# Seven-product keys and values from the third pair of tiles, with the weight sums made earlier and the later key features scaled on GpSimd

## The chip, the cores and the metric

One core of a Trainium2 chip runs the kernel. The metric is the device time of one execution in microseconds. In the profile PE is TensorE (matmuls), DVE is VectorE, ACT is ScalarE, POOL is GpSimd and SP is SyncE, which here issues most DMAs; PEld is TensorE's loading of weights. Each engine works through its own queue of instructions in order, and waits at an instruction until the semaphores that it names have come.

## The reference

The input `x` has 2048 tokens of 512 features. Everything is float32.

```python
xn = (x - mean(x)) / sqrt(var(x) + 1e-5)               # per token

# A: linear attention with learned features, 32 heads of 16
q, k, v = split(xn @ wqkv)
pq, pk  = q @ w_phi, k @ w_phi                          # per head
phi_q   = concat(softmax(pq), softmax(-pq))             # 32 features a head
phi_k   = concat(softmax(pk), softmax(-pk))
kv, z   = sum over tokens of phi_k^T v, and of phi_k    # per head
s       = ((phi_q @ kv) / (phi_q . z + 1e-6)) @ wo

# B: gated feed-forward, F = 1376
gate = xn @ W_gate
ffn  = (gate * (gate > 0) * (xn @ W_up)) @ W_down

out = x + s * silu(ffn)
```

## The kernel before

**Products.** A float32 factor is split into a high and a low half, and each product is made of three matmuls: low by high, high by low, high by high (`mm3`). A projection of one tile of 128 tokens has four slices of the 512 inner rows, so 12 matmuls of 128x512.

**Phase 1.** The 16 tiles of tokens are read, normalised, transposed into `XT`, projected to keys and values, turned into key features, and summed into the state. Tiles 0 and 1 are set up one by one in a loop over `n in range(2)`. Then `pair(m)` runs for m = 1 to 7 with the tiles n = 2m and n + 1; below, "pair 3" is m = 3. On TensorE a pair is: keys of n, values of n + 1, the transposes of a later tile (`pxT`), a query product (`pq`), the state products (`pkv<-ek,v`) of the tiles n - 2 and n - 1, keys of n + 1, values of n, transposes, another query product.

**Two forms of a pair.** Four projections in the plain form are 48 matmuls. From the pair FIRST on, the four are made together by a scheme of seven products of half the inner depth, 7 blocks of 6, so 42 matmuls. The blocks use sums of token blocks (S1 to S4, which GpSimd and VectorE make for the feed-forward part anyhow: tiles `sb`, `xf`, `XT`) and four sums of the weights, `T[0]` to `T[3]`. Their order in a pair is: `py` from A11 by the weights themselves, `pz` from S1 by `T[0]`, `px` from S2 by `T[1]`, the rest of `py`, `px` from S3 by `T[2]`; then, after the state products, `px` from A22 by `T[3]` and the rest of `pz`. Between the blocks ScalarE copies partial sums out (`va`, `vb`) and VectorE adds them back into `v`.

**The weight sums.** `t_prep` defines the steps that make `T[0]` to `T[3]`. A step has a name of four characters: the engine (g GpSimd, s ScalarE), the operation (c combines weights in place, h copies the high half, l subtracts it to leave the low half), the number of the sum, and a slice. There are 20 steps on GpSimd, each a 128x512 operation writing `wvr`, `t`, `l` or `th`, and 8 on ScalarE. The dictionary PLAN places them: `t_steps(m, where)` stands at fixed places of `pair`, and the place decides where the step falls in its engine's queue. Pair 0 in PLAN is the set-up of tile 1.

**Key features.** `features_k(n, e, p, engine)` sums the exponentials `ek` on VectorE (`sm`), takes the reciprocal, and multiplies `ek` by it. Without an engine the reciprocal goes into the PSUM tile of the keys and VectorE multiplies; with one the reciprocal goes into a tile `rc` in SBUF and that engine multiplies. It is called twice in a pair: at its start for tile n - 1, and in its middle for tile n, just ahead of GpSimd's low halves of S1 and S3 (`sums_lo`) for tile n + 3.

**The sum of the features.** `features_split(n)` adds `ek` into `zacc` by a DMA that accumulates, 512 KB, issued by GpSimd. Each of these is made to wait, in GpSimd's queue, for the landing of the one before. There are 15. The state product of a tile needs its `ek` scaled; the products of `zacc` with `ones`, in the second tile of the feed-forward part, need the last accumulate landed.

**Order around it.** Everything is issued in the written order on each engine (line 60, the helper that records each instruction, so that nearly all instructions show as L60). A planner, `pace`, slips the preparation of the feed-forward weights (`f_prep`: tiles `rawg`, `wab`, `tab`, `wa`, `wb`, `wc`, `wd`, `fdh`, `fdl`) into the pairs 5 to 7 by its own estimate of free time: tile 2 first, then tiles 0 and 1; each product is stored to memory (`ws`) and fetched again later. In the pairs 1 to 4 SyncE spills parts of `XT` (`xts`). Behind pair 7 the feed-forward part begins with tile 0, and takes most of the rest of the time.

Of the kernel before, what the change touches and what calls it, by code (L numbers as in the profile page):

```python
# [33 lines left out]
         *(((q, j), (q + 1, j)) for q in (6, 4) for j in range(2)), ((3, 0), (3, 1))]  # L34
LAST = [2 * q + j for q in QUERIES[1] for j in range(2)][-3:]
AHEAD, AT = (2,), (10,)
FIRST = 4
PLAN = {(1, "end"): "gc51", (2, "start"): "gc01", (2, "sums"): "gc50 gc00", (2, "scaled"): "gc11", (2, "split a"): "sh01 gc21", (2, "turned"): "sh20", (2, "end"): "gc10 sh00 sh11", (3, "split b"): "sh21", (3, "sums"): "gl20 gc20", (3, "scaled"): "gl01", (3, "split a"): "gl00 gc31", (3, "turned"): "gl21 sh10 gc30", (3, "end"): "gl10", (4, "start"): "gl11 gc40 gc41", (4, "split b"): "sh30 sh31 gl31", (4, "sums"): "gl30"}

START = (14, 15)  # L40
WO_WITH = (4, 5, 6, 7)
# [119 lines left out]
def layer_kernel(ctx: ExitStack, tc: tile.TileContext, x, wkT, wqT, wv, wo, wf, cst, out):  # L161
    pace = Clock()
    nc = InOrder(tc, pace)
# [4 lines left out]
    def ps(shape=(P, 512), name="ps"):  # L168
        return pp.tile(list(shape), F32, tag="ps", name=name)
# [7 lines left out]
    def u2(shape, name, dt=F32):  # L177
        return sb.tile(list(shape), dt, tag="u2", bufs=B2, name=name)

    def small(n, name, bufs=3):  # L180
        return sb.tile([P, n], F32, tag=name, bufs=bufs, name=name)
# [7 lines left out]
    def add(engine, o, a, b, op=ALU.add):  # L189
        engine.tensor_tensor(o, a, b, op=op)  # L190
# [9 lines left out]
    def mm3(ps_out, w, m, ks, first=True, last=True):  # L200

        n = len(ks)
        for i, k in enumerate(ks):
            (wh, wl), (mh, ml) = w(k), m(k)
            mm(ps_out, wl, mh, first and i == 0, False)
            mm(ps_out, wh, ml, False, False)
            mm(ps_out, wh, mh, False, last and i == n - 1)
            if i < n - 1:
                pace.pump()
# [7 lines left out]
    def groups(e):  # L217
        return e.rearrange("p h s f -> p (h s) f")
# [23 lines left out]
    def rows(w):  # L242
        return lambda k: w[k]
# [35 lines left out]
    def norm_stats(*ns, bn=True):  # L279

        rs = small(2, "lr", 3)
        for k, n in enumerate(ns):
            STAT[n] = (norm_bn if k and bn else norm_sums)(n, rs[:, k:k + 1]), rs[:, k:k + 1]
        RS[ns] = rs

    def norm_scale(*ns):
        for n in ns:
            STAT[n][0][0]()
        rs = RS.pop(ns)[:, :len(ns)]
        nc.gpsimd.tensor_tensor(rs, rs, mhalf[:, :len(ns)], op=ALU.pow)  # L290

    def norm_apply(n):
        (_, m, sign), rs = STAT.pop(n)
        bias = small(1, "lb")
        nc.vector.tensor_scalar(bias, m, sign, rs, op0=ALU.mult, op1=ALU.mult)
        nc.scalar.activation(XN[n], XN[n], AF.Identity, bias=bias, scale=rs)
# [17 lines left out]
    def cols(n):  # L314
        i = order[n][1]
        return slice(i * P, (i + 1) * P)
# [56 lines left out]
    def xt_cols(n):  # L373
        a, c = A21 if n % 2 else A11, cols(n)
        return lambda k: (XT[:, a + k // 2, 0, k % 2, c], XT[:, a + k // 2, 1, k % 2, c])
# [3 lines left out]
    def spill_x(n):  # L379
        nc.sync.dma_start(xt_spill[:, :, :, :, cols(n)].rearrange("p c s k t -> p (c s k) t"),  # L380
                          f32(XT[:, 1:, :, :, cols(n)].rearrange("p c s k t -> p (c s k) t")))
# [37 lines left out]
    def exponents(pk):  # L419

        pkv_ = pk.rearrange("p (h f) -> p h f", f=DH)
        e = u4((P, H, 2, DH), "ek")
        mx = sb.tile([P, 2, H], F32, tag="mx", bufs=2, name="mx")
        nc.vector.tensor_reduce(mx[:, 0, :], pkv_, op=ALU.max, axis=AX.X)
        nc.vector.tensor_reduce(mx[:, 1, :], pkv_, op=ALU.min, axis=AX.X)
        for s in range(2):
            top = mx[:, s, :].unsqueeze(2).to_broadcast([P, H, DH])
            a, b = (top, pkv_) if s else (pkv_, top)
            nc.vector.tensor_tensor(e[:, :, s, :], a, b, op=ALU.subtract)
        return e  # L430
# [4 lines left out]
    def by_head(t, perm=False):  # L435

        return t.rearrange("p (c g f) -> p g c f" if perm else "p (g c f) -> p g c f", c=4, f=DH)
# [23 lines left out]
    def features_k(n, e, p, engine=None):  # L461

        sm = small(64, "sm", 2)
        nc.vector.tensor_reduce(sm, groups(e), op=ALU.add, axis=AX.X)
        rc = small(64, "rc", 2) if engine else p[:, 0:64]
        nc.vector.reciprocal(rc, sm)
        (engine or nc.vector).tensor_tensor(groups(e), groups(e), rc.unsqueeze(2).to_broadcast([P, 64, DH]), op=ALU.mult)
        EK[n] = e
# [5 lines left out]
    def features_split(n):  # L474
        phi = EK.pop(n)
        if n:
            nc.gpsimd.dma_start(zacc, flat(phi), accum_op=ALU.add)
        else:
            nc.sync.dma_start(zacc, flat(phi))
        PHI[n] = phi  # L480
# [636 lines left out]
    def t_steps(m, where):  # L1117
        for what in PLAN.get((m, where), "").split():
            STEPS[0](what)
# [66 lines left out]
    def pair(m):  # L1186

        n, c = 2 * m, cols(2 * m)
        at[0] = n

        def block(p, s, w, first):
            mm3(p, lambda k: (XT[:, s, 0, k, c], XT[:, s, 1, k, c]), rows(w), range(2), first)
            pace.pump()
        if m <= NP // 2:
            pace.later(4, lambda: spill_x(n - 1))
        seven = m >= FIRST
        py = ps(name="pk")
        if seven:
            block(py, A11, WK[:2], True)
            px = ps(name="pk")  # L1200
            nc.scalar.activation(px, py, AF.Copy)
        else:
            mm3(py, xt_cols(n), rows(WK), range(KD))
        if m > 1:
            features_k(n - 1, *EB.pop(), engine=MULT[1])
        t_steps(m, "start")
        pz = ps(name="pv")
        if seven:
            block(pz, S1, T[0], True)
            block(px, S2, T[1], False)  # L1210
            va = u2((P, D), "va")
            nc.scalar.activation(va, px, AF.Copy)
        else:
            mm3(pz, xt_cols(n + 1), rows(WV), range(KD))
        if m == 1:
            norm_apply(n + 4)
        else:
            features_split(n - 1)
        t_steps(m, "split b")
        news = [k for k in (n + 5, n + 6) if k < N]  # L1220
        if news:
            norm_stats(*news, bn=m > 2)
        if seven:
            block(py, A12, WK[2:], False)
        ea = exponents(py)
        if seven:
            block(px, S3, T[2], False)
            vb = u2((P, D), "vb")
            nc.scalar.activation(vb, px, AF.Copy)
            VH[n + 1] = u2((P, D), "v")  # L1230
            add(nc.vector, by_head(VH[n + 1], True), by_head(pz), by_head(vb))
        else:
            vb = pz
        t_steps(m, "sums")
        if news:
            norm_scale(*news)
        t_steps(m, "scaled")
        pace.pump()
        at[0] = n + 1
        if n + 3 < N:  # L1240
            t = turn(n + 3)
        exp_all(ea)
        if not seven:
            features_v(n + 1, vb)
        if n + 3 < N:
            turned(*t)
            sums_more(n + 3)
            sums_hi(n + 3, 0)
            if n + 7 < N:
                load_x(n + 7)  # L1250
        t_steps(m, "mid")
        query(n - 1)
        features_k(n, ea, py, engine=MULT[0])
        if n + 3 < N:
            sums_hi(n + 3, 1)
            sums_lo(n + 3)
        for k in news:
            norm_apply(k)
        pace.pump()
        features_split(n)  # L1260
        t_steps(m, "split a")
        kv_products(n - 2)
        kv_products(n - 1)
        pace.pump()
        if seven:
            block(px, A22, T[3], False)
        else:
            px = project(n + 1, WK, "pk")
        eb = exponents(px)
        if seven:  # L1270
            block(pz, S4, WV[2:], False)
            VH[n] = u2((P, D), "v")
            add(nc.vector, by_head(VH[n], True), by_head(pz), by_head(va))
        else:
            va = project(n, WV, "pv")
        if n + 4 < N:
            t = turn(n + 4)
            if n + 8 < N:
                load_x(n + 8)
        exp_all(eb)  # L1280
        t_steps(m, "turned")
        if n + 4 < N:
            turned(*t)
        if not seven:
            features_v(n, va)
        EB.append((eb, px))
        query(n)
        t_steps(m, "end")
        pace.pump()

    EB, MULT = [], [None, None]
    for m in range(1, NP):
        pair(m)
    features_k(N - 1, *EB.pop())
# [211 lines left out]
```

## Time and profile before

| | before |
|---|---|
| time, median of 3 runs | 549.36 us (548.53 to 551.20) |
| the profiled execution's own time | 548.27 us |
| its span | 546.5 us |
| PE busy | 540.7 us (99%) |
| POOL busy | 344.2 us (63%) |
| DVE busy | 377.2 us (69%) |
| ACT busy | 259.9 us (48%) |
| accumulates into `zacc` | 15, 512 KB each, median 5.9 us from issue to landing |

The span is the stretch between the first and the last instruction of the profiled execution; what lies around it, 1.8 us, is not in the trace. A row of a timeline gives the start in the span, the duration, the engine, the line, the operation with output and inputs, and in brackets the idle time of the engine ahead of it with what ended that. A duration can overlap the next instruction's, so the pitch of an engine is read from starts and ends of neighbours. A row of the windows gives for one stretch its length, then for each engine the busy time and the number of instructions, then TensorE's granted clock (1.00 is full), the DMA engines' share and GB/s.

### The profile page before, as it was taken

Reading aid. Unit: us, or ns where it says so; the run is one execution under the profiler, and the core shown is the slowest. Engines: PE = TensorE matmul, PEld = TensorE weight load, DVE = VectorE, ACT = ScalarE, POOL = GpSimd, SP = SyncE. Lnnn points to the kernel's source line nnn. Section 1 sums busy time; section 2 is a strip of 40 time slices with the busy share of each in tenths; the row PEclk is TensorE's granted clock in tenths of the full one; section 3 lists DMA queues with packets and bytes.
Section 4 is the critical chain, followed back from the end, with each engine's and each line's share of the span. In section 5 each row is a group of like instructions: output and inputs, shape, how many; then the busy total and the mean of one; then the engine's idle time right before and its main releaser. Section 6 shows DMA issues by size and latency. Waiting matters only on the chain.

```text
span 546.5 us, 9074 instructions
## 1 busy us (share of the span) xinstructions
PE 540.7 (99%) x3158; PEld 441.5 (81%) x3158; DVE 377.2 (69%) x582; ACT 259.9 (48%) x457; POOL 344.2 (63%) x311
## 2 busy tenths in 40 slices
PE   8999999999999999999999999999999999999997
PEld 8888887888877888878888888887877887878886
DVE  5978685897759486889833442899999494924323
ACT  3887666674622656455443241334354545342510
POOL 1665879477851999899976235262365765842591
PEclk9999999999999999999999999999999999999999
DMA  8349977659998548789696998792664734657073
GB/s 280 149 161 304 263 184 185 158 125 290 288 328 319 196 136 306 288 290 313 233 341 255 404 415 324 251 349 77 217 210 135 272 113 146 239 188 276 0 232 116
DMA packets 77518, 127.81 MB, mean 234 GB/s; under 512 B 6816, under 2 KB 29216, under 8 KB 76576
## 3 DMA queue, kind: packets, MB, share of 16 engines
q1 hardware_dynamic: 75168, 119.30, 62.1%
q0 software_dynamic: 2160, 7.87, 7.5%
q8 instruction: 25, 0.41, 0.3%
q14 instruction: 21, 0.17, 0.1%
q10 hardware_dynamic: 144, 0.07, 0.0%
HBM read 70.32 MB, written 48.50 MB: 217 GB/s over the span
## 4 chain that ended last, share of the span: by engine, by line
PE 84%; DVE 6%; POOL 5%; issue 2%; DMA 1%; ACT 1%; SPq 1%; ACTq 0%; POOLq 0%
PE py L60 20%; PE pd L60 9%; PE pa L60 9%; PE pb L60 8%; PE pso L60 8%; PE pk L60 7%; PE pq L60 6%; PE pc L60 6%; PE pv L60 4%; POOL l L60 2%; PE pnum L60 1%; PE pfold L60 1%; PE pkv L60 1%; PE pxT L60 1%; DMA wb<-ws 1%
## 5 line engine op out<-in xcount | busy, mean ns | idle before, releaser
L60 PE MATMUL py<-fdh,hl 128*128 128x512 f32 x176 | 68.9, 392 | 0.0
L60 PE MATMUL py<-fdl,hh 128*128 128x512 f32 x176 | 68.5, 389 | 0.0
L60 PE MATMUL py<-fdh,hh 128*128 128x512 f32 x176 | 68.5, 389 | 0.0
L60 PE MATMUL pa<-XT,wa 128*128 128x512 f32 x264 | 67.2, 390 | 0.0
L60 PEld LDWEIGHTS pa<-XT,wa 128*128 128x128 f32 x264 | 49.4, 188 | 10.7 <-issue 0.4
L60 DVE TENSOR_TENSOR y<-py,y 128x512 f32<-128x512 f32 x40 | 27.5, 689 | 37.0 <-PE py L60 36.9
L60 POOL TENSOR_TENSOR hl<-t,hh 128x512 fp32r<-128x512 f32 x16 | 20.7, 1296 | 39.0 <-ACT hh L60 38.5
L60 POOL TENSOR_TENSOR y<-y,ys 128x512 f32<-128x512 f32 x24 | 30.9, 1292 | 17.5 <-ACT ys L60 17.1
L60 PE MATMUL pq<-XT,wqh 128*128 128x512 f32 (+1 forms) x144 | 40.5, 367 | 0.0
L60 PEld LDWEIGHTS py<-fdh,hl 128*128 128x128 f32 x176 | 33.0, 188 | 8.4 <-issue 1.2
L60 PEld LDWEIGHTS py<-fdh,hh 128*128 128x128 f32 x176 | 33.0, 188 | 6.9
L60 PEld LDWEIGHTS py<-fdl,hh 128*128 128x128 f32 x176 | 33.0, 188 | 6.7
L60 POOL TENSOR_TENSOR ez<-eq,zB 128x1024 f32<-128x1024 f32 x16 | 38.4, 2403 | 0.1
L60 ACT ACTIVATE hh<-t 128x512 fp32r<-128x512 f32 x16 | 10.1, 632 | 52.8 <-DVE t L60 51.9
L60 PE MATMUL pd<-XT,wd 128*128 128x512 f32 x132 | 34.0, 393 | 0.1
L60 PE MATMUL pb<-XT,wb 128*128 128x512 f32 x132 | 33.9, 391 | 0.0
L60 PE MATMUL pd<-XT,wc 128*128 128x512 f32 x132 | 33.9, 391 | 0.0
L60 PE MATMUL pc<-XT,wb 128*128 128x512 f32 x132 | 33.5, 389 | 0.0
L60 PE MATMUL pk<-wkh,XT 128*128 128x512 f32 x96 | 32.8, 395 | 0.0
L60 POOL TENSOR_TENSOR ol<-of,oh 128x512 fp32r<-128x512 f32 (+1 forms) x13 | 19.8, 1551 | 20.3 <-ACT oh L60 20.3
L60 POOL TENSOR_TENSOR hl<-e,hh 128x512 fp32r<-128x512 f32 x6 | 7.8, 1292 | 35.0 <-ACT hh L60 26.9
L60 PEld LDWEIGHTS pd<-XT,wd 128*128 128x128 f32 x132 | 24.4, 188 | 6.4 <-DVE t L60 1.4
(185 smaller groups left out, 1432.2 us busy)
## 6 DMA issues: line engine op xcount, KB each, us to landing
zacc<-ek POOLq DMA_DIRECT2D x15, 512.0 KB, 5.9
xts<-XT SPq DMA_DIRECT2D x4, 1792.0 KB
XT<-xts SPq DMA_DIRECT2D x7, 1024.0 KB
wa<-ws SPq DMA_DIRECT2D x24, 256.0 KB
wb<-ws SPq DMA_DIRECT2D x24, 256.0 KB
wc<-ws SPq DMA_DIRECT2D x24, 256.0 KB
rawg<-wf SPq DMA_DIRECT2D x22, 256.0 KB
ws<-wc SPq DMA_DIRECT2D x22, 256.0 KB
```

Of the source, the lines that this page charges most:

```text
L60: return self.tc.keep_in_program_order(op(*a, **k))
```

## The change

It has three parts. FIRST goes from 4 to 3, so pair 3 takes the seven-product form. PLAN is replaced: the same 20 and 8 steps now run from the set-up of tile 1 to the middle of pair 3, where they ran from the end of pair 1 to the middle of pair 4. And SWAP is new: in the pairs behind m = 3 both calls of `features_k` multiply on GpSimd, 8 multiplies in all; the last tile's call behind the loop stays on VectorE.

```diff
-FIRST = 4
-PLAN = {(1, "end"): "gc51", (2, "start"): "gc01", (2, "sums"): "gc50 gc00", (2, "scaled"): "gc11", (2, "split a"): "sh01 gc21", (2, "turned"): "sh20", (2, "end"): "gc10 sh00 sh11", (3, "split b"): "sh21", (3, "sums"): "gl20 gc20", (3, "scaled"): "gl01", (3, "split a"): "gl00 gc31", (3, "turned"): "gl21 sh10 gc30", (3, "end"): "gl10", (4, "start"): "gl11 gc40 gc41", (4, "split b"): "sh30 sh31 gl31", (4, "sums"): "gl30"}
+FIRST, SWAP = 3, 3
+PLAN = {(0, "turned"): "gc51", (1, "split b"): "gc50", (1, "sums"): "gc01", (1, "scaled"): "gc11", (1, "mid"): "gc21", (1, "split a"): "gc00 sh01 gl01", (1, "turned"): "gc10", (2, "split b"): "sh20 sh11", (2, "sums"): "sh00 gc20", (2, "scaled"): "sh21 gl00", (2, "split a"): "gl20", (2, "turned"): "sh10 gc30 gl11", (2, "end"): "gl21 gl10", (3, "start"): "gc31 gc40 gc41", (3, "split b"): "sh30", (3, "sums"): "sh31 gl30 gl31"}
...
         if m > 1:
-            features_k(n - 1, *EB.pop(), engine=MULT[1])
+            features_k(n - 1, *EB.pop(), engine=MULT[m > SWAP][1])
...
-        features_k(n, ea, py, engine=MULT[0])
+        features_k(n, ea, py, engine=MULT[m > SWAP][0])
         if n + 3 < N:
             sums_hi(n + 3, 1)
             sums_lo(n + 3)
...
-    EB, MULT = [], [None, None]
+    EB, MULT = [], [(None, None), (nc.gpsimd, nc.gpsimd)]
```

In the built order of instructions TensorE has six matmuls fewer, all in pair 3. VectorE has eight multiplies fewer and two additions more, GpSimd eight multiplies more, ScalarE one copy more, net. The order of GpSimd's queue differs from the set-up of tile 1 to the first feed-forward tile; from there on it is the same.

## The prediction

> **What bounds the kernel now.** I read the page first, then the chain, then the waits of TensorE, and then the timelines of TensorE and GpSimd over the first 172 us, where everything lies that the change touches.
>
> ```profile
> span 546.5 us, 9074 instructions
> PE 540.7 (99%) x3158; PEld 441.5 (81%) x3158; DVE 377.2 (69%) x582; ACT 259.9 (48%) x457; POOL 344.2 (63%) x311
> ...
> PE 84%; DVE 6%; POOL 5%; issue 2%; DMA 1%; ACT 1%; SPq 1%; ACTq 0%; POOLq 0%
> ```
>
> TensorE is busy for 540.7 of 546.5 us. The end therefore moves in two ways only: by the matmuls that are issued, and by new idle time in front of one. The other engines count where TensorE waits for them. The waits of TensorE between 20 and 172 us are this one line:
>
> ```profile
> PE pk L60 <- POOL l L60: 0.3, 1, 0.3
> ```
>
> It is the low half of a weight sum, made on GpSimd, in the first pair that uses the seven products (pair 4).
>
> Half a per cent, 2.75 us, is about what a measurement of this kernel can tell from no change. The profiled execution took 548.27 us: 546.5 of span and 1.8 around it. That is 1.09 below the median of the runs shown, 549.36. I make the sum in the profiled execution and add 1.09 at the end.
>
> **1. Six matmuls fewer in pair 3.** TensorE's work by pair, from the windows (length, then busy time of PE):
>
> ```profile
> 66.81:85.35 18.54, 18.54 (x146) 15.15 (x144) 14.79 (x26) 12.92 (x24) 15.51 (x16) 1.00 0.86 224
> 85.35:103.15 17.80, 17.53 (x140) 13.87 (x138) 13.49 (x25) 10.98 (x20) 15.42 (x15) 1.00 0.60 141
> 103.15:120.33 17.18, 17.18 (x140) 14.03 (x138) 15.55 (x25) 11.50 (x20) 8.30 (x10) 1.00 0.51 124
> ```
>
> Pair 3 has 146 matmuls and takes 18.54 us; pair 5, with the seven products, has 140 and takes 17.18. Six matmuls are 1.36 us, 0.227 each, at a granted clock of 1.00. Pair 3 gets the seven-product form: **-1.36 us**. The copies by ScalarE and the additions by VectorE that come with it find idle time: ScalarE is busy for 12.92 of the 18.54 us, VectorE for 14.79.
>
> **2. The old stall goes.** Pair 4 has the same 140 matmuls as pair 5 and takes 0.62 longer. It is here (PE, and the POOL row it waits for):
>
> ```profile
> 86.36 3.04 POOL L60 TENSOR_TENSOR l<-wvr,h 128x512 fp32r<-128x512 f32 x2
> ...
> 89.46 0.50 PE L60 MATMUL pk<-l,XT 128*128 128x512 f32 x1 [0.27 <-POOL l L60]
> ```
>
> GpSimd's `l` ends at 89.40 and the matmul starts at 89.46. In the changed kernel all weight sums are done in pair 3, so pair 4 finds them: **-0.62 us**. What is late next in pair 4 is nothing of the weights.
>
> **3. A new stall in pair 3.** All 20 of GpSimd's weight steps must now be done before pair 3 uses them, some 18 us sooner. They share GpSimd's queue with the accumulates of `zacc`, and each accumulate waits in that queue for the landing of the one before.
>
> ```profile
> 33.63 1.30 POOL L60 TENSOR_TENSOR XT<-xf,XT 128x512 fp32r<-128x512 f32 x1
> ...
> 45.42 0.87 POOL L60 DMA_DIRECT2D zacc<-ek  x1
> ...
> 55.95 0.88 POOL L60 DMA_DIRECT2D zacc<-ek  x1 [6.96 <-ACT ek L60]
> 56.55 1.59 POOL L60 TENSOR_TENSOR t<-wvr 128x512 f32<-128x512 f32 x1
> 58.22 1.29 POOL L60 TENSOR_TENSOR wvr<-wvr,wkh 128x512 f32<-128x512 f32 x1
> 59.48 0.73 POOL L60 TENSOR_TENSOR lr<-lr,mhalf 128x2 f32<-128x2 f32 x1
> 60.18 1.28 POOL L60 TENSOR_TENSOR wvr<-wvr,wkl 128x512 f32<-128x512 f32 x1
> 61.43 1.42 POOL L60 TENSOR_TENSOR xf<-xf,sb 128x256 f32<-128x256 f32 x2
> 62.82 1.28 POOL L60 TENSOR_TENSOR XT<-sb,XT 128x512 fp32r<-128x512 f32 x1
> ...
> 43.77 0.62 SPq L60 DMA_DIRECT2D xts<-XT  x1
> ...
> DMA to landing us min/median/max: 4.4/5.9/10.0
> ```
>
> From these: a step of 128x512 takes 1.25 us from end to end, `xf` 1.40, `lr` 0.70; the step behind an accumulate ends 2.19 after the accumulate starts (55.95 to 58.14). From 34.93, where `XT` ends, the new order is: step, accumulate of tile 1 with the step behind it, six steps of 1.25, `lr`, `xf` and one more step. That is 1.25 + 2.19 + 7 x 1.25 + 0.70 + 1.40 = 14.3: the accumulate of tile 2 starts at 49.2 (before 45.42). Three steps follow and end at 53.9; then GpSimd reaches the accumulate of tile 3 and waits. With the median landing, 5.9, tile 2 has landed at 55.1, and this accumulate starts some 0.6 later, as in the row at 55.95 (45.42 + 10.0 = 55.4): 55.7. Behind it stand step, `lr`, step, `xf`, two `XT`: 2.19 + 0.70 + 1.25 + 1.40 + 2.50, to 63.8; then the accumulate of tile 4 with the first of five steps, 2.19 + 4 x 1.25, to 70.9. The last of these five is the `l` of the second weight sum for the inner rows that TensorE uses first.
>
> ```profile
> 66.81 0.39 PE L60 MATMUL pk<-wkh,XT 128*128 128x512 f32 x1
> ...
> 69.53 0.39 PE L60 MATMUL pv<-wvh,XT 128*128 128x512 f32 x1
> 69.75 0.39 PE L60 MATMUL pv<-wvl,XT 128*128 128x512 f32 x1
> ```
>
> Two blocks of six matmuls come first; the third block starts at 69.53, and its second matmul, at 69.75, wants that `l`. Stall: 70.9 + 0.06 - 69.75, **+1.2 us**. With a landing of 4.4 the steps are done at 69.4 and there is no stall; with 10.0 the accumulate starts at 59.8, the `l` ends at 75.0 and the stall is 5.3. I take the median: the landing of 10.0 is that of the accumulate at 45.42 itself, issued 1.7 us behind a spill of `xts`, and the moved one comes 5.4 us behind that spill. The fourth sum follows at 78 against a use near 79: hidden by about a microsecond.
>
> **4. Eight multiplies to GpSimd.**
>
> ```profile
> L60 POOL TENSOR_TENSOR ez<-eq,zB 128x1024 f32<-128x1024 f32 x16 | 38.4, 2403 | 0.1
> L60 DVE TENSOR_TENSOR ek<-ek,pk 128x1024 f32<-128x1024 f32 x14 | 17.1, 1221 | 0.5
> L60 DVE TENSOR_TENSOR eq<-eq,qr 128x1024 f32<-128x1024 f32 x16 | 19.1, 1213 | 0.1
> ```
>
> VectorE is rid of 8 x 1.22 = 9.8 us, worth nothing, as TensorE does not wait for it in this stretch. GpSimd has no such operation on `ek`; the nearest row is `ez`, the same shape, 2.40 us: 8 x 2.40 = 19.2 us more over pairs 4 to 7. GpSimd is busy for 15.42 of 17.80 us in pair 4 and loses its weight steps there; in pair 5 for 8.30 of 17.18. The multiply stands ahead of the `XT` low halves that the next pair's second block needs 1.36 us after its start, and the accumulate stands behind both. Those two pairs have room for 4.8 us each. Pair 6, with the feed-forward weights' steps, is the tight one.
>
> ```profile
> 118.73 0.83 POOL L60 DMA_DIRECT2D zacc<-ek  x1
> 119.37 1.78 POOL L60 TENSOR_TENSOR rawg<-rawg 128x256 f32<-128x256 f32 x2
> 121.12 2.69 POOL L60 TENSOR_TENSOR wab<-rawg,wab 128x256 fp32r<-128x256 f32 x3
> 123.77 1.28 POOL L60 TENSOR_TENSOR wc<-rawg,wc 128x512 fp32r<-128x512 f32 x1
> 125.02 0.73 POOL L60 TENSOR_TENSOR wd<-rawg,wd 128x256 fp32r<-128x256 f32 x1
> ...
> 134.40 0.86 POOL L60 DMA_DIRECT2D zacc<-ek  x1
> ...
> 142.28 0.83 POOL L60 DMA_DIRECT2D zacc<-ek  x1
> ...
> 158.26 0.88 POOL L60 DMA_DIRECT2D zacc<-ek  x1 [1.44 <-DMA zacc<-ek]
> ...
> 138.37 0.39 PE L60 MATMUL pv<-h,XT 128*128 128x512 f32 x1
> ...
> 156.04 0.65 PE L60 MATMUL pkv<-ek,v 128*32 128x64 f32 x32
> ...
> 169.21 0.64 PE L60 MATMUL pkv<-zacc,ones 128*32 128x256 f32 x8
> ```
>
> The accumulate at 118.73 moves 2.4 later, to 121.1. Behind it: `rawg` to 123.4, a multiply to 125.8, three `wab` to 128.4, an accumulate with `wc` behind it to 130.6, VectorE's `sb` (which waits for this `wc`) to 131.4, `xf`, `wd`, a multiply, two `XT`: 1.40 + 0.70 + 2.40 + 2.50, to 138.4. TensorE wants it at 138.37 to 138.6: **0** (0 to 0.4).
>
> **5. The last accumulates.** The one of tile 12 now comes at 138.4, not 134.40, and the feed-forward steps that stood behind the last three now stand between them. The landings of those issued at 142.28, 150.06 and 158.26 were
>
> ```profile
> DMA to landing us min/median/max: 7.2/7.2/7.2
> DMA to landing us min/median/max: 7.6/7.6/7.6
> DMA to landing us min/median/max: 8.6/8.6/8.6
> ```
>
> I take 7.2 for each, half way between the median of all, 5.9, and the last one's 8.6. Tile 13 then goes at 138.4 + 7.2 + 0.6 = 146.2. Four `tab`, two `wa` (0.7 each, as the `wd` row at 125.02; the first ends 1.6 after the accumulate starts, 2.19 less the difference to 1.25), `wb`, `wc` and the multiply of tile 14: 1.6 + 5 x 0.7 + 2 x 1.25 + 2.40, to 156.2. TensorE wants it at 156.04: about even. Tile 14 goes at 156.2 and has landed at 163.4; tile 15 goes at 164.0 (before 158.26) and has landed at 171.2. TensorE wants it at 169.21: **+2.0 us**. With three landings of 5.9 the multiply ends at 154.9 and tile 15 has landed at 167.3: nothing. With 8.6 for the last two, 174.0: 4.8. The chain and TensorE both move with pair 3's stall, so the difference stays.
>
> **The sum.** -1.36 - 0.62 + 1.2 + 0 + 2.0 = +1.2 us: 549.5 in the profiled execution, **550.6** against the median.
>
> The Trainium skill, "DMA: Bandwidth & Descriptors", section "Anatomy of one DMA", gives a transfer that GpSimd issues as about 2.0 us plus its bytes at 436 GB/s, an estimate of 3.2 us for these 512 KB. By it both stalls would vanish and the time would be that of the second rival; the trace speaks against it, since the shortest of the 15 landings took 4.4 us and the longest 10.0.
>
> **Rivals.**
> The last accumulates are hidden after all (landings under 6 us, because the stores of feed-forward weights beside them move back too): -1.36 - 0.62 + 1.2 = -0.8, so 548.6. For it: most landings before 134 us were 4.4 to 5.9. Against: all three behind 142 us were longer. Chance 0.20.
>
> Neither stall: -1.98, so 547.4. It needs a landing under 4.7 in pair 2 too. Chance 0.13.
>
> Slower: the accumulates of tiles 14 and 15 take 8.6 each, as the one at 158.26 did, and TensorE stands 4.8 us in the second feed-forward tile, at the products of `zacc` with `ones`: +4.0, so 553.4. It decides from 1.6 us more stall than I forecast, that is from 16.0 for both landings together. For it: the landings grew from 7.2 to 8.6 along this stretch. Chance 0.18.
>
> Slower in pair 3: tile 2's accumulate takes 10 us like the one that it replaces: 5.3 of stall in place of 1.2, so 554.7. Chance 0.06.
>
> VectorE is held up by GpSimd's multiplies: a VectorE instruction with both operands in SBUF would stand for up to 2.40 us behind each. Two a pair, 4.8 us, less the 2.44 us of the multiplies that VectorE is rid of, against 1.6 us of idle time in pair 5: 0.8 a pair, some 3 us over four pairs, so 553.6. Against it: `eq<-eq,qr`, both operands in SBUF, takes 1213 ns beside a GpSimd that is busy for 63%, and `ek<-ek,pk`, one operand in PSUM, takes 1221. Chance 0.03. The Trainium skill, "SBUF — State Buffer", section "Who interferes with whom", has such a lock between VectorE with two SBUF inputs and a reading GpSimd; the two rows do not show it.
>
> That the matmuls are not saved is no rival: the built order has six fewer.
>
> **How the numbers follow.** Forecast 0.40 (548.8 to 552.3: 0.35 within half a per cent of 549.36, that is up to 552.1, and 0.05 above). Hidden end 0.20 within. Neither stall 0.13: 0.10 within, 0.03 faster, if pairs gain a little beside. The three slow cases 0.27. Faster 0.03, same 0.65, slower 0.32. The range goes from 547.3, just under the case of no stall, to 553.6, which leaves out pair 3's long landing and the upper edge of the slow end.
>
> **What would show it.** Six matmuls fewer, and pair 3 at 17.2 us plus a stall; a wait of TensorE for POOL `l` near 69.7 of about 1.2 us and none in pair 4; `ek` multiplies on POOL of 2.4 us; the last accumulate at about 164 and TensorE waiting for it in front of `pkv<-zacc,ones`. The prediction is wrong if TensorE shows a wait elsewhere in pairs 1 to 7, or if it is slower without one of these two stalls.

## The result: slower by 0.8%, at a place that the prediction had passed by

| | before | changed |
|---|---|---|
| time, median of 6 runs | 549.43 us (548.53 to 551.20) | 554.25 us (553.02 to 555.75) |
| profiled execution | 548.27 us | 553.32 us |
| span | 546.5 us | 551.5 us |

The ratio is 1.0081, 95% interval 1.0057 to 1.0105. The forecast was 550.6 us, between 547.3 and 553.6; the time lies above the range.

The head of the page of the changed kernel, and TensorE's two longest waits (engine and tile that waited, engine and tile waited for, us in all, times, longest):

```profile
span 551.5 us, 9075 instructions
PE 541.6 (98%) x3152; PEld 442.1 (80%) x3152; DVE 371.7 (67%) x576; ACT 259.8 (47%) x458; POOL 359.9 (65%) x319
```

```profile
PE pc L60 <- DVE e L60: 2.8, 1, 2.8
PE pk L60 <- POOL l L60: 1.8, 1, 1.8
```

The six matmuls are gone (3158 to 3152), and the multiplies have moved (POOL 344.2 to 359.9 us busy). TensorE has these two waits in place of the old one of 0.3. The second in the list is the one in pair 3. The first stands in the second tile of the feed-forward part, behind all that the change touches, and it costs more than it says. TensorE there, before and changed:

```profile
171.96 1.52 PE L60 MATMUL pd<-XT,wc 128*128 128x512 f32 x6
173.39 1.66 PE L60 MATMUL pc<-XT,wc 128*128 128x512 f32 x6
174.89 1.52 PE L60 MATMUL pa<-XT,wa 128*128 128x512 f32 x6
```

```profile
172.84 1.52 PE L60 MATMUL pd<-XT,wc 128*128 128x512 f32 x6
177.18 2.93 PE L60 MATMUL pc<-XT,wc 128*128 128x512 f32 x6 [2.82 <-DVE e L60]
179.90 1.69 PE L60 MATMUL pa<-XT,wa 128*128 128x512 f32 x6
```

From `pd` to `pa` it was 2.93 us and is 7.06, so 4.1 us are lost. The wait is 2.8 of it; the six matmuls behind it run at half the clock. In the windows of the changed kernel the third figure from the end is the granted clock:

```profile
177.18:179.90 2.72, 2.72 (x6) 2.15 (x7) 2.34 (x4) 0.43 (x1) 0.00 (x0) 0.50 1.06 398
```

The whole difference of the two spans, 5.1 us, by TensorE's timelines matched row by row: 0.7 in the set-up ahead of pair 1, 0.2 net in the pairs 3 and 4, and 4.3 in the second feed-forward tile. From there to the end the distance stays at 5.2 to 5.1. The 0.7 of the set-up can't be put down to the change: in two of the kernels below whose set-up is that of the kernel before, it is 0.2 and 1.1.

**Why VectorE is late there.** The last accumulates and what stands behind them on GpSimd, before and changed:

```profile
150.06 0.88 POOL L60 DMA_DIRECT2D zacc<-ek  x1 [2.05 <-DVE mx L60]
...
155.26 1.55 POOL L60 TENSOR_TENSOR fdl<-rawd,fdh 128x512 fp32r<-128x512 f32 x1
```

```profile
143.41 0.88 POOL L60 DMA_DIRECT2D zacc<-ek  x1 [1.22 <-DMA zacc<-ek]
...
151.11 1.94 POOL L60 TENSOR_TENSOR ek<-ek,rc 128x1024 f32<-128x1024 f32 x1
153.35 0.87 POOL L60 DMA_DIRECT2D zacc<-ek  x1 [0.30 <-POOL ek L60]
...
161.63 0.89 POOL L60 DMA_DIRECT2D zacc<-ek  x1 [4.00 <-DVE u L60]
162.24 1.86 POOL L60 TENSOR_TENSOR tab<-rawg,tab 128x256 f32<-128x256 f32 x2
...
165.45 1.28 POOL L60 TENSOR_TENSOR wb<-tab,wb 128x512 fp32r<-128x512 f32 x1
166.69 1.29 POOL L60 TENSOR_TENSOR wc<-tab,wc 128x512 fp32r<-128x512 f32 x1
167.93 0.74 POOL L60 TENSOR_TENSOR wd<-rawg,wd 128x256 fp32r<-128x256 f32 x1
168.63 1.28 POOL L60 TENSOR_TENSOR fdl<-rawd,fdh 128x512 fp32r<-128x512 f32 x1
```

Tile 14's multiply comes at 151, behind most of the steps of the first feed-forward tile, so its accumulate goes at 153.35 and not at 150.06. The next accumulate has to wait for that landing, 7.7 us later: GpSimd stands for 4.0 us. (The `DVE u` in the bracket ended at 161.31. But the landing came at 161.07, and the accumulate follows it by 0.56 us, as it does in the kernels below with the plan alone, 0.57, and the multiplies alone, 0.56. So the landing is what it needed.) The steps of the second feed-forward tile, which before were through at 156.8, run from 162 to 170, but for the first two. That does two things. ScalarE, before and changed:

```profile
162.39 0.38 ACT L60 ACTIVATE kvacc<-pkv 128x256 f32<-128x256 f32 x1 [3.42 <-PE pkv L60]
```

```profile
163.31 0.63 ACT L60 ACTIVATE wb<-tab 128x512 fp32r<-128x512 f32 x1 [3.47 <-POOL tab L60]
...
165.50 0.36 ACT L60 ACTIVATE kvacc<-pkv 128x256 f32<-128x256 f32 x1
```

ScalarE's queue has `wb` and `wc`, which need those steps, ahead of `kvacc`, which comes at 165.50 in place of 162.39. And VectorE's four small copies into `kvt`, before and changed:

```profile
164.27 0.92 DVE L60 COPY kvt<-kvT 32x128 f32<-32x128 f32 x4
```

```profile
166.38 3.62 DVE L60 COPY kvt<-kvT 32x128 f32<-32x128 f32 x4
170.03 0.70 DVE L60 TENSOR_TENSOR pc<-pc,u 128x512 f32<-128x512 f32 x1
...
176.44 0.68 DVE L60 TENSOR_TENSOR e<-pc,u 128x512 f32<-128x512 f32 x1
```

The same four copies take 3.62 us in place of 0.92. In the kernel before VectorE is idle for 0.84 us (0.64 and 0.20) between the copies and the `e` that TensorE's `pc` needs; here it works without a pause to that `e` at 176.44, and `pc` waits for it. Two theories were put to the test: L, that the copies are held up by a GpSimd at work beside them; and Q, that VectorE is late by the queues alone.

### The profile page after: what moved, and what is told of

It is laid out like the page before. It is cut to its first block, busy times and chain, and to the rows that moved or that the text cites. A ratio compares the mean times of both kernels' runs of the same rounds, so it can differ in the third digit from the quotient of the medians.

```text
span 551.5 us, 9075 instructions
## 1 busy us (share of the span) xinstructions
PE 541.6 (98%) x3152; PEld 442.1 (80%) x3152; DVE 371.7 (67%) x576; ACT 259.8 (47%) x458; POOL 359.9 (65%) x319
## 4 chain that ended last, share of the span: by engine, by line
PE 80%; DVE 7%; POOL 6%; ACT 3%; issue 2%; DMA 1%; DVEq 0%; ACTq 0%; POOLq 0%
PE py L60 20%; PE pa L60 9%; PE pd L60 9%; PE pb L60 8%; PE pso L60 8%; PE pk L60 7%; PE pc L60 5%; PE pq L60 5%; PE pv L60 3%; PE pnum L60 1%; PE pfold L60 1%; POOL l L60 1%; POOL XT L60 1%; PE pkv L60 1%; DVE eq L60 1%
## 5 line engine op out<-in xcount | busy, mean ns | idle before, releaser
L60 DVE TENSOR_REDUCE mx<-pk 128x32 f32<-128x512 f32 x32 | 20.6, 684 | 22.7 <-PE pk L60 22.7
L60 PE MATMUL pk<-wkh,XT 128*128 128x512 f32 x88 | 30.2, 395 | 0.0
L60 PEld LDWEIGHTS pq<-XT,wqh 128*128 128x128 f32 x144 | 26.0, 189 | 4.3
```

The costliest lines, as they stand in the source:

```text
L60: return self.tc.keep_in_program_order(op(*a, **k))
```

## The experiments

Each kernel ran on the same chip as runs of the kernel before; the ratio is against those, with its 95% interval.

**The plan alone.** The changed kernel with the multiplies on VectorE.

```diff
-    EB, MULT = [], [(None, None), (nc.gpsimd, nc.gpsimd)]
+    EB, MULT = [], [(None, None), (None, None)]
```

> The changed kernel with all key multiplies left on VectorE: seven products from pair 3 and the new plan alone. Theory M (the multiplies on GpSimd delay the last accumulates and the feed-forward steps, and that costs the 4.2 us at pc of the second feed-forward tile): the kvt copies take 0.9 us, TensorE does not wait at pc, and of the two known terms only pair 3 is left: its stall of 2.1 stays, pair 4's 0.6 is gone, six matmuls fewer: 549.4 - 1.4 - 0.6 + 2.1 = 549.5. Rival (the moved weight steps and transfers delay the late part too): the wait at pc stays, about 554.

Measured: 550.84 us, ratio 1.0004 (0.9984 to 1.0024). Theory M holds, the rival does not: no wait at `pc`, copies 0.92 us, the stall in pair 3 at 2.1. Two waits of TensorE for VectorE's `t` later in the feed-forward part, 0.9 together, were not expected. Matched row by row, TensorE falls 1.8 us further behind between 230 and 260 us, more than the 1.3 us by which the time exceeds the forecast; the cause stays open.

**The multiplies alone.** The kernel before with `MULT[m > SWAP]` and SWAP = 3.

> The kernel before with the eight multiplies on GpSimd and nothing else. Theory M: the wait at pc of the second feed-forward tile comes, 4.2 us with the half clock behind it: about 553.6; the stall in pair 4 may grow by some tenths. Rival (it takes the plan and the multiplies together): 549.4.

Measured: 557.60 us, ratio 1.0130 (1.0087 to 1.0174). The wait at `pc` came, and was dearer (3.2 us and the half clock, 4.9 in all). The stall in pair 4 was mis-sized by far: not some tenths more but 2.15 us in place of 0.3, since a multiply now stood between two `l` of the weight sums:

```profile
87.89 1.78 POOL L60 TENSOR_TENSOR l<-wvr,h 128x512 fp32r<-128x512 f32 x1
89.15 2.41 POOL L60 TENSOR_TENSOR ek<-ek,rc 128x1024 f32<-128x1024 f32 x1
91.04 1.74 POOL L60 TENSOR_TENSOR l<-wvr,h 128x512 fp32r<-128x512 f32 x1
...
92.83 0.50 PE L60 MATMUL pk<-l,XT 128*128 128x512 f32 x1 [2.15 <-POOL l L60]
```

So the multiplies lose 1.3% on their own. Matched row by row, this kernel falls 2.3 us back in the pairs 3 and 4 and the changed one 0.2: the plan, which has no weight steps in pair 4, saves the difference.

**One multiply back.** The changed kernel with the multiply of tile 14 alone on VectorE.

```diff
-        features_k(n, ea, py, engine=MULT[m > SWAP][0])
+        features_k(n, ea, py, engine=MULT[SWAP < m < 7][0])
```

> The changed kernel with one multiply back on VectorE, that of tile 14, which stands in GpSimd's queue behind the steps of the first feed-forward tile and ahead of the last two accumulates. Theory M (that multiply makes the accumulate of tile 14 late, and GpSimd then stands waiting for its landing with the next feed-forward steps behind): tile 14's accumulate goes at about 150 and tile 15's at about 158, GpSimd is through before the kvt copies, they take 0.9, and the wait at pc is gone: 550.1. Rival (the other seven multiplies have already made the queue late): the accumulates stay at 153 and 161 and the time at 554.2.

Measured: 549.36 us, ratio 0.9990 (0.9978 to 1.0002). One multiply of eight carries the whole loss: 554.25 to 549.36. The accumulates of the tiles 14 and 15:

```profile
151.32 0.85 POOL L60 DMA_DIRECT2D zacc<-ek  x1
...
158.75 0.87 POOL L60 DMA_DIRECT2D zacc<-ek  x1 [1.64 <-ACT wd L60]
```

Some 2 to 3 us sooner is enough: GpSimd is through at 165.5, the copies take 1.22 us from 165.06, and TensorE's only long wait left, but for the one at its start, is pair 3's.

**The copies as another operation.** The changed kernel; VectorE writes `kvt` as a sum over one element. The index and the rearrangement of `kvt` are shortened to `...`.

```diff
-            nc.vector.tensor_copy(kvt[r, ...], kvT[r, :, 0:4:3, :])
+            nc.vector.tensor_reduce(kvt[r, ...], kvT[r, :, 0:4:3, :].unsqueeze(4), op=ALU.add, axis=AX.X)
```

> The changed kernel with the four copies into kvt done by VectorE as sums over one element: same engine, same data, same place, another operation. Theory L (the copies are held up by GpSimd working beside them, 3.6 in place of 0.9 us): the four take about 1 us, VectorE reaches e some 2.7 us sooner, TensorE's wait at pc falls from 2.8 to 0.1 and the half clock behind it does not come: about 550.1. Theory Q (VectorE is late because ScalarE's kvacc is late behind wb and wc, which wait for GpSimd): the four still take about 3.6 and the time stays at 554.2.

Measured: 551.24 us, ratio 1.0021 (0.9996 to 1.0045).

```profile
165.92 0.45 DVE L60 STREAM_TRANSPOSE kvT<-kvacc 128x256 f32<-128x256 f32 x1 [1.48 <-ACT kvacc L60]
166.40 1.15 DVE L60 TENSOR_REDUCE kvt<-kvT 32x128 f32<-32x128 f32 x4
```

The start is the same as in the changed kernel (166.38) and GpSimd works beside it as there (`wb` from 165.47, `wc` from 166.73), but the four take 1.15 us, not 3.62. The wait at `pc` falls to 0.7 us and the clock stays at full. So theory L explains some 3 us of the time: by the rows the second feed-forward tile costs 0.8 us here in place of 4.3. The wait of 0.7 that is left is for the most part theory Q's, the late `kvacc`; the sums are themselves 0.23 longer than undisturbed copies. The two delays add up on VectorE ahead of one `e`, and its 0.84 us of idle time takes up part of the first of them, so their shares depend on which is counted first.

**GpSimd busy beside the copies, in the kernel before.**

```diff
         nc.vector.transpose(kvT, kvacc)
+        beside = sb.tile([P, 256], F32, tag="beside", bufs=1, name="beside")
+        for _ in range(6):
+            nc.gpsimd.tensor_tensor(beside, kvacc, kvacc, op=ALU.add)
```

> The kernel before with six additions on GpSimd (128x256, 0.7 us each, of kvacc into a scratch tile) that start when kvacc is there and run beside the transpose and the four kvt copies; nothing waits for them but the reuse of kvacc's slot. Theory L (the copies are held up by a GpSimd that works beside them): the four copies take 2.5 to 3.6 us in place of 0.92, VectorE reaches e about 2 us later, TensorE waits 1 us at pc: about 550.5. Theory Q (queues alone): 0.92 and 549.4.

Measured: 550.08 us, ratio 1.0014 (0.9994 to 1.0034). The time alone decides nothing; the rows do:

```profile
163.24 4.06 POOL L60 TENSOR_TENSOR beside<-kvacc 128x256 f32<-128x256 f32 x6 [4.03 <-ACT kvacc L60]
...
164.18 0.43 DVE L60 STREAM_TRANSPOSE kvT<-kvacc 128x256 f32<-128x256 f32 x1
164.65 2.73 DVE L60 COPY kvt<-kvT 32x128 f32<-32x128 f32 x4
```

With `kvacc` in time and nothing moved, the copies take 2.73 us, until GpSimd is done at 167.3. The transpose beside the same GpSimd takes 0.43 as ever. TensorE's wait at `pc` is 0.7.

The rows of the single copies show how they are held up, which the sum of the four hides. In the changed kernel they take 0.43, 1.23, 0.68 and 1.23 us (0.22 each before) and end at 166.81, 168.06, 168.75 and 169.99; GpSimd's `wb`, `wc`, `wd` and `fdl` end at 166.73, 167.98, 168.67 and 169.91. Each copy ends 0.08 us behind one GpSimd operation. It is the same for the four copies here (0.08 or 0.09 behind four of the six additions) and with the multiplies alone. With tile 14's multiply back, only the first copy meets a GpSimd operation, and ends 0.09 behind it; the other three take 0.22 each. So the copies do not run slowly: each stands until the GpSimd operation that is under way has ended, and the next copy meets the next operation.

**The low half earlier in pair 3.** The changed kernel with `(2, "turned"): "sh10 gl10 gl11", (2, "end"): "gl21 gc30"`.

> The changed kernel with the low half of the second sum's first slice two steps earlier in GpSimd's queue, and a combining step later. Theory: the pair-3 stall is only that step's place: it ends at about 69.1 against a use at 70.4, the stall of 2.1 goes, and the time falls by 2.1 at most, to 552.2, with the wait at pc unchanged. Rival (the wait at pc is set by GpSimd's own late queue, not by TensorE): what is won in pair 3 is lost at pc, 554.2.

Measured: 553.21 us, ratio 1.0056 (1.0037 to 1.0075). A miss: the stall at `l` is gone, but the fourth sum, whose first step had been moved back for it, is late in its place. Pair 3 takes 18.7 us in place of 19.3, and 0.5 of that is lost again in pair 4: behind it TensorE is only 0.1 us better off than in the changed kernel. The intervals of the two ratios overlap.

```profile
79.03 1.21 PE L60 MATMUL pk<-th,XT 128*128 128x512 f32 x4 [0.43 <-ACT vb L60]
80.97 0.73 PE L60 MATMUL pk<-th,XT 128*128 128x512 f32 x2 [0.73 <-POOL th L60]
```

Pair 3 is held by the length of GpSimd's queue, not by the order in it.

**Three steps on VectorE.** So the queue was made shorter: multiplies on VectorE, the low half earlier, and three combining steps taken from GpSimd, where VectorE had time.

```diff
-(2, "turned"): "sh10 gc30 gl11", (2, "end"): "gl21 gl10", (3, "start"): "gc31 gc40 gc41"
+(2, "turned"): "sh10 gl10 gl11", (2, "end"): "gl21 gc30", (3, "start"): "vc31 vc40 vc41"
...
+    EB, MULT = [], [(None, None), (None, None)]
```

> Seven products from pair 3 with all key multiplies on VectorE, the low half of the second sum's first slice earlier, and three combining steps of the fourth sum (one of the third pair's start for each of c31, c40, c41) on VectorE in place of GpSimd. Theory P (what pair 3 loses is the length of GpSimd's queue): GpSimd is rid of 3.75 us ahead of the fourth sum, so the stalls at the second and the fourth sum go and the two savings stay: 549.4 - 1.4 - 0.6 = 547.4, up to 548.2 with some tenths left. Rival (the pair stalls on something else each time that one wait is taken away, ScalarE's copies among them): about 549.4, no gain.

Measured: 548.17 us, ratio 0.9969 (0.9950 to 0.9988). It beats both kernels. In its profile the only wait of TensorE left is the one at the start, 1.1 us at `pidle`, which every kernel here has.

Matched row by row with the kernel before, TensorE gains 1.8 us between pair 3 and the end of pair 4 (from 1.08 behind to 0.74 ahead), which is the 1.4 + 0.6 of the prediction but for 0.2.

**Both together.** The same with the multiplies on GpSimd, all but tile 14's.

> Both repairs together: the plan with the three combining steps on VectorE, and the key multiplies of pairs 4 to 7 on GpSimd but for tile 14's. It asks whether the multiplies are worth anything on GpSimd once nothing waits for them. Theory V (VectorE is not on the path in pairs 4 to 7, so its 1.2 us a multiply are worth nothing): the same as with all multiplies on VectorE, 548.2. Rival (VectorE's relief lets TensorE through somewhere): under 547.5.

Measured: 547.62 us, ratio 0.9966 (0.9951 to 0.9981). The same as without them, by ratio 0.9966 against 0.9969: once nothing waits for GpSimd, moving 8.5 us of work off VectorE is worth nothing that can be measured.

## Why the prediction was wrong, point by point

1. *Six matmuls fewer, -1.36.* Right. In the kernel with three steps on VectorE, which has no stall, pair 3 takes 17.18 us, as pair 5 does.
2. *The old stall goes, -0.62.* Right: TensorE does not wait in pair 4 of the changed kernel, and the pair takes 17.18 us.
3. *A new stall in pair 3, +1.2.* Right place, right row, mis-sized: 2.0. Two neighbouring matmuls start 2.24 us apart, at 70.24 and 72.48, in place of 0.23; the row below counts 1.85 of it as idle. The accumulate of tile 2 went at 49.64 (forecast 49.2) and took 7.1 us to land, not the median 5.9, so that of tile 3 went at 57.30 (55.7), 0.56 behind that landing; the `XT` in its bracket is not what it waited for. TensorE itself came 0.7 later.

```profile
57.30 0.88 POOL L60 DMA_DIRECT2D zacc<-ek  x1 [2.70 <-ACT XT L60]
...
70.67 1.75 POOL L60 TENSOR_TENSOR l<-wvr,h 128x512 fp32r<-128x512 f32 x1
...
72.48 0.50 PE L60 MATMUL pk<-l,XT 128*128 128x512 f32 x1 [1.85 <-POOL l L60]
```

4. *Multiplies, 0.* The price was over-stated (1.9 us each from end to end, not the 2.40 of `ez`), and TensorE waited for nothing in the pairs 5 to 7, as forecast.
5. *The last accumulates, +2.0, at the products of `zacc` with `ones`.* This is the step that failed. Its order was right: tile 14's multiply makes tile 14's accumulate late, 153.35 (forecast 156.2), and tile 15's waits for it, 161.63 (forecast 164.0). But its end was wrong. The products at 170.09 did not wait: tile 15 landed after 7.6 us, at 169.2. One landing had been mis-sized: tile 12's took 4.8 us, not 7.2, so tile 13's accumulate went at 143.41 and not at 146.2, and with the 7.2 all behind it would, by these rows, have come some 2.4 us later: an estimate of 1.5 us of wait at the products. And the price was paid by what stands behind the accumulate of tile 15 on GpSimd. I followed the accumulate to its one reader and not the steps of the second feed-forward tile behind it: whom they keep waiting (ScalarE's `wb`, with `kvacc` behind it), and what they then run beside (VectorE's copies). It came to 4.3 us: 2.8 of wait, and 1.5 from a clock that I had taken as 1.00 throughout.

The slow rival of that step had the right tile, a price near the true one (4.8 of stall), and the wrong reader; its sign of recognition, landings that add up to 16.0, did not come (7.7 + 7.6). That its time, 553.4, lies near the measured 554.25 is luck.

The rival of VectorE held up by GpSimd got 0.03, and VectorE held up by GpSimd is what cost most, though at other instructions and beside other GpSimd work than the rival named. The reading that spoke against it was wrong: `qr` is a tile of PSUM (the kernel makes it with `ps`), so neither `eq<-eq,qr` nor `ek<-ek,pk` has both operands in SBUF, and the two rows test nothing. A row of the kernel before that does bear on it was passed by:

```profile
21.87 0.99 DVE L60 TENSOR_SCALAR xt<-xt,bm,br 128x512 f32<-128x512 f32 x1
```

This operation goes from SBUF to SBUF and has a GpSimd `xf` beside it until 22.58; the same operation at 20.22 takes 0.54 us. No experiment changed that one, so the cause of its 0.99 us is not shown. The copies too go from SBUF to SBUF, with one operand tile. The Trainium skill, "SBUF — State Buffer", section "Who interferes with whom", names both kinds, says that a copy can run in a mode that takes the port pair shared with GpSimd, and that whichever comes second stands until the first is done, while a `tensor_reduce` on this chip never does. For these copies the runs agree: 0.92 us alone, 3.62 and 2.73 beside GpSimd with each copy ending just behind a GpSimd operation, and 1.15 as a reduce beside GpSimd. I had cited the section for its half on two SBUF operands and not looked for the other half in the kernel. The half on two operands is met once, in the kernel with three steps on VectorE: beside VectorE's `t<-wkh,wvr` at 70.37 GpSimd's `l` at 70.48 takes 1.73 us, the `l` ahead of it 1.30. One such row is a hint and no more.

The estimate of 3.2 us for a landing, from the Trainium skill, "DMA: Bandwidth & Descriptors", section "Anatomy of one DMA", did not hold for these accumulates: tile 2 took 7.1 us, tile 14 7.7 and tile 15 7.6.

## What to carry to other kernels

When a change makes an engine's queue late, follow every instruction behind the late one, not only the late one's own reader: who waits for each, what stands behind that waiter in its own queue, and what the work now runs beside. A few small copies on VectorE that are hidden while GpSimd rests can cost four times their length when GpSimd's work slides over them, one GpSimd operation for each copy. A shorter queue (three steps on the idle engine) and one multiply left where it was gave 0.3% where the same change as written lost 0.8%. An operation moved off an engine that nothing waits for gains nothing, and has to be priced where it lands.

## What the runs showed of the hardware

A pause of TensorE of a few microseconds can cost more than itself. With those of 2.5, 2.8 and 3.2 us at `pc` (the low half earlier, the changed kernel, the multiplies alone) the granted clock fell to 0.50. With pauses of up to 2.15 us (pair 4 with the multiplies alone) it stayed at 1.00. Each time the lower clock lasted 3.41 us. Here are that stretch and the 3.41 us ahead of it in the changed kernel, and a stretch of 3.41 us with most of a pause of 2.06 in it, with the plan alone; the figure behind the length is what TensorE was busy:

```profile
173.38:176.79 3.41, 0.98 (x5) 0.47 (x3) 3.38 (x7) 0.63 (x3) 1.40 (x2) 1.00 1.04 361
176.79:180.20 3.41, 3.02 (x7) 2.44 (x8) 2.79 (x6) 0.82 (x1) 0.00 (x0) 0.50 1.03 387
```

```profile
68.52:71.93 3.41, 1.78 (x8) 1.13 (x6) 2.05 (x4) 0.58 (x1) 3.41 (x5) 1.00 1.08 278
```

In the 3.41 us ahead of the three falls TensorE was busy for 0.98 us (changed), 0.91 (the low half earlier) and 0.42 (the multiplies alone). The clock records of the three traces begin with the full clock at 6.12, 6.56 and 6.40 us, and the falls come 170.67, 170.67 and 174.08 us later, which is 50, 50 and 51 times 3.413. In these traces, then, the clock changes on a grid of such stretches. On that grid the pause of 2.15 us in pair 4 lies half in one stretch and half in the next, and TensorE is busy for 2.15 and 2.32 us of them. So these traces do not give a limit for the length of a pause: stretches with 0.98 us of work or less were followed by the lower clock, those with 1.78 or more were not, and a pause counts by how it falls on them. No run here moves a pause on the grid and nothing else.

In the changed kernel the lower clock made six matmuls take 2.72 us in place of 1.36. The Trainium skill, "TensorE: Matmul & The Clock Gate", Part 1, has the clock halve after an idle window of about 3.4 us that runs freely; the 3.41 us agree, but here a window with 0.98 us of work in it was enough.
